# Large loads asked for by GpSimd's software queue, one packet per DMA engine, in place of SyncE's hardware queue

## The chip, the cores and the metric

The kernel runs on one core of a Trainium2 chip. The metric is the device time of one execution in microseconds (us): 1309.09 us for the kernel before, the median of 3 runs (1309.06 to 1309.27). Times inside an execution are counted from the first instruction of the span that the profiler recorded.

## The reference, cut to what matters

Decode step of a block with cached keys and values, B = 4 batches, 32 heads, 4096 cached positions, head size 128, model width 512, all in float32:

```python
q = (x @ wq) as (b, h, 1, d)
scores = einsum("bhqd,bhkd->bhqk", q, k_cache) * 128 ** -0.5
o = einsum("bhqk,bhkd->bhqd", softmax(scores), v_cache)
a = o as (b, 1, 4096) @ wo
ffn = (gelu(x @ w_gate) * (x @ w_up)) @ w_down        # F = 1792
g = sigmoid((x * gate_w).sum(-1))
return g * a + (1 - g) * ffn
```

The two caches are 268 MB each and every byte of them is read once; with the weights some 565 MB come in, and 8 KB go out.

## The kernel before

The work is cut into NT = 32 turns, one for each batch and group of four heads. A turn needs one K tile and one V tile, each of 128 partitions by 64 KB (8.4 MB): a partition holds 128 consecutive cache rows of one head. All of it lives in one big SBUF tensor, `big`, in which the K tiles of two turns overlap in a quarter of their rows and V has one place.

In turn i, VectorE (DVE) multiplies the shared quarter of the K tile by the query (`products(i, True)`, L384) and sums it (`sums(i, True)`, L390). That quarter is then free, and K of turn i+1 is asked for. DVE goes on with the other three quarters (L384 and L390 again, three times as long), then the row maximum (`soft_max`). ScalarE makes the exponentials (L402). TensorE multiplies V of the turn before by them (`pv(i - 1)`, L416), after which V of turn i is asked for.

Ahead of the turns stands an opening: `wq` (8.4 MB) and K of turn 0 are asked for by SyncE (SP), `x` and `gate_w` (8 KB each) by ScalarE's queue. GpSimd (POOL) makes an identity (`ident`, L298 and L299); TensorE turns `x` with it (`x_turn`, L312), DVE spreads it into `xT` (L317), TensorE projects it with `wq` (`q_project`, L330), DVE picks what it needs out of it (L347 to L368), TensorE and ScalarE spread it (L372, L374) as `qb`, and only then can turn 0 start. `w_gate` and `w_up` (3.7 MB each, `load_f`) go to the place of `wq` in `big`, and are asked for when `q_project` has read it. After the turns come `w_down`, `wo` and the last projections (L497, L505), and SP stores the result in two parts (L616).

Order and waits are set by a small class, `Plan`: each step is recorded with what it reads and writes, in program order, and each engine plays its own steps in that order, with semaphore waits worked out from the overlaps. A load waits on its issuing engine for whoever read its destination last. A load counts its completion on a semaphore of its lane, and its reader waits for that.

The opening loads are played inside a critical section of the tile framework, and then the framework's context is closed, ahead of everything else:

```python
with tc.tile_critical(sync_engine=mybir.EngineType.Pool, no_gpsimd_drain=True):
    plan.play(plan.steps[:opening])
tc.close()
```

Closing the context (its instructions bear the line L625) puts a drain into every engine's program, which is an instruction that holds the engine until its own older work is complete, and a barrier that all five engines enter and leave together. The rows of POOL named `ISA [waits barrier...gather]` below belong to it. So no engine begins `ident`, `ones`, `x_turn` or anything later before each engine has come to that barrier.

Of the kernel before, what the change touches and what calls it, by code (L numbers as in the profile page):

```python
# [19 lines left out]
class Plan:  # L20
# [18 lines left out]
    def add(self, engine, emit, reads=(), writes=(), lane=None, unit=1):  # L39
        lane = lane or engine  # L40
        self.units[lane] = unit
        row = self.by_lane.setdefault(lane, [])
        step = Step(lane, engine, emit, self.turn if engine in self.loops else None)
        step.at = len(row)
        need = {}
        for accesses, writing in ((reads, False), (writes, True)):
            for name, lo, hi in accesses:
                for other, a, b, wrote in self.past.get(name, ()):
                    if a < hi and lo < b and (wrote or writing):
                        if other.lane == engine and engine == "pe":  # L50
                            continue
                        if other.lane == engine and not wrote:
                            continue
                        need[other.lane] = max(need.get(other.lane, -1), other.at)
        seen = self.seen[engine]
        for l, n in sorted(need.items(), key=lambda x: -len(self.by_lane[x[0]])):
            if seen.get(l, -1) >= n:
                continue
            other = self.by_lane[l][n]
            other.asked = True  # L60
            step.waits[l] = n
            seen[l] = n
            for k, v in self.knew[other].items():
                seen[k] = max(seen.get(k, -1), v)
        step.waits = {l: n for l, n in step.waits.items()
                      if not any(self.knew[self.by_lane[m][k]].get(l, -1) >= n for m, k in step.waits.items() if m != l)}
        self.knew[step] = dict(seen)
        self.knew[step][lane] = step.at
        if row and lane == engine:
            for k, v in self.knew[row[-1]].items():  # L70
                if k != lane:
                    self.knew[step][k] = max(self.knew[step].get(k, -1), v)
        for accesses, writing in ((reads, False), (writes, True)):
            for name, lo, hi in accesses:
                old = self.past.get(name, [])
                if writing:
                    old = [x for x in old if not (lo <= x[1] and x[2] <= hi)]
                self.past[name] = old + [(step, lo, hi, writing)]
        row.append(step)
        self.steps.append(step)  # L80
        return step
# [51 lines left out]
def tile_gated_mix(tc: tile.TileContext, x, kc, vc, wq, wo, w_gate, w_up, w_down, gate_w, out):  # L133
    nc = tc.nc
# [108 lines left out]
    add = plan.add  # L243
    V, A, T, G = nc.vector, nc.scalar, nc.tensor, nc.gpsimd
# [11 lines left out]
        return g if plan.k is None else plan.k  # L256

    def load(dst, src, writes, lane):
        return add("sp", lambda: nc.sync.dma_start(dst, src), (), writes, lane=lane, unit=16)

    def load_kv(kind, i):
        src = (vc, kc)[kind == "k"]
        a = KB_ * (i % 2) if kind == "k" else VA if i < NT - 1 else 0
        s = src[i % B, HT * (i // B):HT * (i // B) + HT].rearrange("h (p r) d -> (h p) (r d)", p=PH)
        load(place(a, TW), s, [z(a, TW)], "vl" if kind == "v" and i == NT - 1 else kind)
# [7 lines left out]
    def load_f(s):  # L273
        load(place((F0, F1)[s], KC * F), (w_gate, w_up)[s].rearrange("(p c) n -> p (c n)", c=KC),
             [z((F0, F1)[s], KC * F)], f"f{s}")

    def load_d():
        load(place(D0, FC * DM), w_down.rearrange("(p i) n -> p (i n)", i=FC), [z(D0, FC * DM)], "k")
# [326 lines left out]
    for h in range(2):  # L605
# [4 lines left out]
        for c, move in ((2 * h + 1, act), (2 * h, dve)):  # L610
            dst, read, write = res[:B, slice(*COLS[c])], [(("acc", "po0")[h], 0, C4)], [("res", *COLS[c])]
# [46 lines left out]
```

## Time and profile before

| what | before |
|---|---|
| median of 3 runs | 1309.09 us |
| span of the profiled execution | 1307.7 us (its time around the span is not listed; the median is 1.4 us above the span) |
| DVE busy | 1158.2 us, 89% |
| TensorE busy | 354.1 us, 27% |
| ScalarE busy | 87.3 us, 7% |
| POOL busy | 0.7 us, 6 instructions |
| SP's DMA queue | 10960 packets, 564.67 MB, 99.7% of 16 engines' time |
| mean DMA rate | 432 GB/s over the span |

A busy share is a mean over the span. The DMA share is that of the 16 DMA engines together; DMA-issuing instructions are not counted as busy, and show in the timeline as `SPq`, the sequencer of SP. In a row of the timeline stand the start, the time taken, the engine, the line, the operation, what it writes and reads, how many instructions are merged in the row, and in brackets how long the engine stood idle before it and what ended that.

### The profile page before, as it was taken

To read this page: it belongs to the slowest core of one execution; us is meant where nothing else is said; L and a number is where in the kernel's file an instruction comes from. 1 tells how busy PE (TensorE), PEld (TensorE's weight loads), DVE (VectorE), ACT (ScalarE), POOL (GpSimd) and SP (SyncE) were. 2 spreads that over 40 slices of the span, in tenths; PEclk is the share of its full clock that TensorE was granted. 3 is DMA by queue.
4 is the path that set the end of the run, shared out by engine and by line. 5 is a ranking of instruction groups with operands and counts; after the bars stand their busy time and mean duration, and the time that the engine had idled before them with its cause. 6 is when DMAs were issued, how large, how long until landed. Compare 5 with 4: busy or idle time off the path is not lost.

```text
span 1307.7 us, 6169 instructions
## 1 busy us (share of the span) xinstructions
PE 354.1 (27%) x2512; PEld 100.8 (8%) x2512; DVE 1158.2 (89%) x303; ACT 87.3 (7%) x291; POOL 0.7 (0%) x6
## 2 busy tenths in 40 slices
PE   3402233201332211322221223321133322122227
PEld 0100001000010000100000000100001000000002
DVE  1899999999899998989989888998989898898992
ACT  0000000000000000000000000000000000000001
POOL 0000000000000000000000000000000000000000
PEclk9656666556666556666656666665666665576669
DMA  9999999999999999999999999999999999999998
GB/s 417 417 446 427 440 439 425 443 425 443 427 441 425 441 425 441 431 437 439 427 443 425 443 427 441 425 441 425 441 431 437 439 427 443 425 443 427 439 428 370
DMA packets 10986, 564.83 MB, mean 432 GB/s; under 512 B 1232, under 2 KB 1752, under 8 KB 1888
## 3 DMA queue, kind: packets, MB, share of 16 engines
q1 hardware_dynamic: 10960, 564.67, 99.7%
q8 instruction: 7, 0.11, 0.0%
q10 hardware_dynamic: 16, 0.02, 0.0%
q14 instruction: 3, 0.02, 0.0%
HBM read 564.67 MB, written 0.01 MB: 432 GB/s over the span
## 4 chain that ended last, share of the span: by engine, by line
DMA 71%; DVE 28%; issue 1%; PE 0%; ACT 0%; SPq 0%; DVEq 0%; POOLq 0%
DMA big<-in_A_k_cache 69%; DVE big L384 14%; DVE sc L390 13%; DMA big<-in_A_wo 2%; PE acc L505 0%; PE wide L497 0%; PE po L505 0%; DVE hT L537 0%; DVE big L535 0%; DVE big L534 0%; DVE big L532 0%; ACT big L511 0%; DVE m L395 0%; ACT big L533 0%; DVE big L530 0%
## 5 line engine op out<-in xcount | busy, mean ns | idle before, releaser
L384 DVE TENSOR_TENSOR big<-big,qb 128x4096 f32<-128x4096 f32 x64 | 556.0, 8687 | 88.8 <-DMA big<-in_A_k_cache 88.8
L390 DVE TENSOR_REDUCE sc<-big 128x32 f32<-128x4096 f32 x64 | 555.9, 8686 | 2.3
L416 PE MATMUL po<-big,PM 128*32 128x512 f32 x2048 | 293.4, 737 | 903.1 <-DMA big<-in_A_v_cache 903.1
L416 PEld LDWEIGHTS po<-big,PM 128*32 128x32 f32 x2048 | 72.3, 132 | 1117.8 <-DMA big<-in_A_v_cache 825.2
L402 ACT ACTIVATE PM<-sc,nb 32x128 f32<-32x128 f32 x128 | 67.2, 525 | 476.5 <-DVE nb L397 429.0
L424 ACT ACTIVATE o<-po 128x512 f32<-128x512 f32 x16 | 9.6, 597 | 443.9 <-PE po L416 443.9
L402 ACT ACTIVATION_READ_ACCUMULATOR PM<-sc,nb 32x1 f32 x128 | 26.1, 204 | 0.0
L374 ACT ACTIVATE qb<-q 128x512 f32<-128x512 f32 x8 | 4.8, 597 | 249.6 <-PE q L372 249.6
L347 DVE TENSOR_TENSOR big<-po,amask 128x512 f32<-128x512 f32 x2 | 1.3, 686 | 19.3 <-PE po L330 19.3
L433 PE MATMUL sm<-o,sel 128*16 128x128 f32 x128 | 15.4, 273 | 5.8 <-ACT o L424 5.8
L330 PE MATMUL po<-big,xT 128*32 128x512 f32 x64 | 10.0, 793 | 18.6 <-DMA big<-in_A_wq 18.6
L518 PE MATMUL q<-big,xT 128*32 128x448 f32 x64 | 10.8, 848 | 13.7 <-DMA big<-in_B_w_gate 11.0
L433 PEld LDWEIGHTS sm<-o,sel 128*16 128x16 f32 x128 | 11.7, 97 | 14.4 <-ACT o L424 13.1
L615 DVE COPY res<-acc 4x144 f32<-4x144 f32 x1 | 0.3, 296 | 13.2 <-PE acc L505 13.2
L372 PE MATMUL q<-QM,hc 128*128 128x512 f32 x16 | 9.9, 706 | 4.2 <-DVE hc L368 4.2
L395 DVE TENSOR_REDUCE m<-sc 128x1 f32<-128x128 f32 x32 | 9.2, 286 | 1.1
L440 DVE RECIPROCAL ri<-sm 16x1 f32<-16x1 f32 x8 | 1.2, 156 | 8.2 <-PE sm L435 8.2
L396 DVE STREAM_TRANSPOSE mt<-m 128x32 f32<-128x32 f32 x32 | 6.8, 212 | 1.1
L397 DVE TENSOR_REDUCE nb<-mt 128x1 f32<-128x32 f32 x32 | 6.0, 186 | 1.1
L497 PE MATMUL wide<-big 128*32 128x512 f32 x46 | 5.6, 596 | 2.3 <-DMA big<-in_A_wo 2.3
L518 PEld LDWEIGHTS q<-big,xT 128*32 128x32 f32 x64 | 3.3, 159 | 20.5 <-issue 20.5
L330 PEld LDWEIGHTS po<-big,xT 128*32 128x32 f32 x64 | 2.7, 139 | 25.1 <-issue 25.1
(74 smaller groups left out, 58.3 us busy)
## 6 DMA issues: line engine op xcount, KB each, us to landing
big<-in_A_wo SPq DMA_DIRECT2D x1, 4096.0 KB, 28.7
big<-in_B_w_gate SPq DMA_DIRECT2D x1, 3584.0 KB, 17.6
big<-in_B_w_up SPq DMA_DIRECT2D x1, 3584.0 KB, 25.8
big<-in_B_w_down SPq DMA_DIRECT2D x1, 3584.0 KB, 19.4
big<-in_A_wo SPq DMA_DIRECT2D x1, 1792.0 KB, 26.3
big<-in_A_wo SPq DMA_DIRECT2D x1, 1280.0 KB, 29.0
big<-in_A_k_cache SPq DMA_DIRECT2D x32, 29.7
big<-in_A_v_cache SPq DMA_DIRECT2D x32, 29.4
```

Of the source, the lines that this page charges most:

```text
L330: last = T.matmul(PO[s][32 * j:32 * j + 32].rearrange("p j d -> p (j d)"), xTf[:, c, :32], w[:, n0:n0 + HB * D], start=c == 0, stop=c == K ...
L372: pe(lambda: T.matmul(q.rearrange("p b d -> p (b d)"), HC.rearrange("p h k -> p (h k)"), QM.rearrange("p b d -> p (b d)"), start=True, sto ...
L384: dve(lambda: V.tensor_tensor(k, k, QB[:, b:b + 1, :].to_broadcast([P, r1 - r0, D]), op=OP.mult), m + t("qb"), m)
L390: dve(lambda: V.tensor_reduce(SC[i % 2][:, r0:r1], k, axis=AX.X, op=OP.add), [z(KA(i) + r0 * D, (r1 - r0) * D)], [(f"sc{i % 2}", r0, r1)])
L395: dve(lambda: V.tensor_reduce(M1[n], SC[n], axis=AX.X, op=OP.max), t(f"sc{n}"), t(f"m1{n}"))
L396: dve(lambda: V.transpose(MT, M1[n].to_broadcast([P, PH])), t(f"m1{n}"), t("mt"))
L397: dve(lambda: V.tensor_reduce(NB[n], MT, axis=AX.X, op=OP.max, negate=True), t("mt"), t(f"nb{n}"))
L402: last = A.activation(PM[:, PZ:].rearrange("p (c m) -> p c m", m=32)[s, :, h:RJ * HT:HT], SC[n][s, :].rearrange("p (c j) -> p c j", j=RJ), ...
L416: last = T.matmul(PO[n][32 * c:32 * c + 32].rearrange("p j d -> p (j d)"), PM[:, m0:m0 + 32], place(VAT(i) + j * N, N), start=b == 0 and j ...
L424: act(lambda: A.activation(O[n], PO[n], AF.Copy), t(f"po{n}"), t(f"o{n}"))
L433: T.matmul(sm[:B * HT, :D], selv[:, j, m0:m0 + B * HT], O[n][:, j, :], start=(n, j) == (0, 0), stop=(n, j) == (N - 1, RJ - 1))
L518: last = T.matmul(q.rearrange("p b d -> p (b d)")[32 * j:32 * j + 32, :FG], xTf[:, c, :32], place((F0, F1)[s] + c * F + j * FG, FG), start ...
```

## The change

The helper through which every large load goes asks on another engine, and with another option:

```diff
     def load(dst, src, writes, lane):
-        return add("sp", lambda: nc.sync.dma_start(dst, src), (), writes, lane=lane, unit=16)
+        return add("pool", lambda: G.dma_start(dst, src, single_packet=True), (), writes, lane=lane, unit=16)
```

`wq`, all K and V tiles, `w_gate`, `w_up`, `w_down` and the pieces of `wo` move from SP's hardware queue to POOL's software queue, where GpSimd's own processors write the descriptors. `single_packet=True` asks that what a load gives one DMA engine, here 8 partitions' rows, forms one packet. `x` and `gate_w` stay on ScalarE's queue and the two stores on SP's. The waits of the loads are the same and move with them. PE, DVE and ACT keep their programs.

POOL's program from the start to `ident` and a little beyond, before (`lane_...` are the semaphores of `Plan`, `..._49` and `barrier_...` those of the framework):

```order
L622 NO_OP
L625 UNCONDITIONAL_BRANCH
L622 NO_OP [waits SP_sequencer_49,Activation_sequencer_49,Pool_sequencer_49]
L625 UNCONDITIONAL_BRANCH
L625 ISA [waits barrier_Pool_Activation_PE_DVE_SP_gather]
L298 MEMSET ident 128x128 [waits barrier_Pool_Activation_PE_DVE_SP_gather]
L299 ISA [waits lane_pool]
L299 AFFINE_SELECT ident<-ident 128x128
```

and the same place after:

```order
L259 DMA big<-in_A_wq 128x16384
L259 DMA big<-in_A_k_cache 128x16384
L622 UNCONDITIONAL_BRANCH
L622 NO_OP [waits Pool_49]
L622 NO_OP [waits Activation_sequencer_49,Pool_sequencer_49]
L625 UNCONDITIONAL_BRANCH
L625 ISA [waits barrier_Pool_Activation_PE_DVE_SP_gather]
L298 MEMSET ident 128x128 [waits barrier_Pool_Activation_PE_DVE_SP_gather]
L299 ISA [waits lane_pool]
L299 AFFINE_SELECT ident<-ident 128x128
L259 DMA big<-in_B_w_gate 128x7168 [waits lane_pe]
L259 DMA big<-in_B_w_up 128x7168
```

POOL now comes to the drain and the barrier of the closed context with two 8.4 MB loads of its own behind it, and the later loads stand behind `ident` on it.

SP's program at the same place before:

```order
L259 DMA big<-in_A_wq 128x16384
L259 DMA big<-in_A_k_cache 128x16384
L622 UNCONDITIONAL_BRANCH
L625 UNCONDITIONAL_BRANCH [waits Pool_49]
L259 DMA big<-in_B_w_gate 128x7168 [waits SP_sequencer_49,Activation_sequencer_49,Pool_sequencer_49,barrier_Pool_Activation_PE_DVE_SP_release,lane_pe]
L259 DMA big<-in_B_w_up 128x7168
L259 DMA big<-in_A_k_cache 128x16384 [waits lane_dve]
L259 DMA big<-in_A_v_cache 128x16384 [waits lane_dve]
```

and all of SP's after:

```order
L654 UNCONDITIONAL_BRANCH
L625 UNCONDITIONAL_BRANCH x2
L616 DMA out<-res 4x288 [waits Activation_sequencer_49,Pool_sequencer_49,Pool_49,barrier_Pool_Activation_PE_DVE_SP_release,lane_fin0]
L616 DMA out<-res 4x224 [waits lane_fin1]
L635 ISA [waits lane_out]
```

What is left on SP are the two stores; each load's own wait (`lane_pe`, `lane_dve`) is POOL's now.

## The prediction

> **What bounds the kernel now.** I read the page's first parts, then the windows, then the timeline at three places.
>
> ```profile
> span 1307.7 us, 6169 instructions
> q1 hardware_dynamic: 10960, 564.67, 99.7%
> 281.00:1200.00 919.00, 238.52 (x1656) 65.46 (x1656) 843.98 (x184) 61.33 (x210) 0.00 (x0) 0.62 1.00 434
> DMA 71%; DVE 28%; issue 1%; PE 0%; ACT 0%; SPq 0%; DVEq 0%; POOLq 0%
> ```
>
> The second row is SP's queue: its packets take 99.7% of the 16 DMA engines' span. The third is a window of 919 us in mid-run, whose last two columns are the DMA share (1.00) and GB/s (434). The kernel is bound by the bytes it moves, and nothing but an idle or a slower DMA stream can lengthen it much. So I ask of each issue: how much was still queued ahead of it when it was made?
>
> ```profile
> 543.39 4.43 DVE L384 TENSOR_TENSOR big<-big,qb 128x4096 f32<-128x4096 f32 x1 [2.14 <-DMA big<-in_A_k_cache]
> 552.18 12.95 DVE L384 TENSOR_TENSOR big<-big,qb 128x12288 f32<-128x12288 f32 x1
> 552.30 0.33 SPq L259 DMA_DIRECT2D big<-in_A_k_cache  x1
> 562.72 9.73 PE L416 MATMUL po<-big,PM 128*32 128x512 f32 x64 [27.38 <-DMA big<-in_A_v_cache]
> 572.51 0.33 SPq L259 DMA_DIRECT2D big<-in_A_v_cache  x1
> 582.04 4.43 DVE L384 TENSOR_TENSOR big<-big,qb 128x4096 f32<-128x4096 f32 x1 [3.13 <-DMA big<-in_A_k_cache]
> ```
>
> One turn lasts 582.04 - 543.39 = 38.65 us. K is asked for at 552.30, while the V ahead of it lands at 562.72: a cover of 10.4 us. V is asked for at 572.51 and the K ahead lands at 582.04: 9.5 us. An issue may be some microseconds slower here without an idle DMA engine. The opening has no such cover everywhere:
>
> ```profile
> 0.89 0.40 SPq L259 DMA_DIRECT2D big<-in_A_wq  x1
> 1.35 0.42 SPq L259 DMA_DIRECT2D big<-in_A_k_cache  x1
> 2.87 0.20 POOL L298 MEMSET ident<- 128x128 f32 x1 [2.43 <-POOLq L625]
> 2.97 0.17 DVE L301 MEMSET ones<- 128x128 f32 x1 [2.97 <-PEq L625]
> 5.39 0.89 DVE L317 COPY xT<-sg 128x128 f32<-128x128 f32 x4
> 10.67 0.68 DVE L320 TENSOR_TENSOR big<-big 4x512 f32<-4x512 f32 x1 [4.39 <-DMA big<-in_gate_w]
> 22.88 9.99 PE L330 MATMUL po<-big,xT 128*32 128x512 f32 x64 [18.58 <-DMA big<-in_A_wq]
> 32.93 0.33 SPq L259 DMA_DIRECT2D big<-in_B_w_gate  x1
> 39.16 0.60 ACT L374 ACTIVATE qb<-q 128x512 f32<-128x512 f32 x1 [35.00 <-PE q L372]
> 42.15 4.43 DVE L384 TENSOR_TENSOR big<-big,qb 128x4096 f32<-128x4096 f32 x1 [5.16 <-DMA big<-in_A_k_cache]
> 51.06 0.33 SPq L259 DMA_DIRECT2D big<-in_A_k_cache  x1
> 59.19 1.45 PE L518 MATMUL q<-big,xT 128*32 128x448 f32 x8 [2.64 <-DMA big<-in_B_w_up]
> 69.48 0.33 SPq L259 DMA_DIRECT2D big<-in_A_v_cache  x1
> 92.16 0.33 SPq L259 DMA_DIRECT2D big<-in_A_k_cache  x1
> 99.17 9.39 PE L416 MATMUL po<-big,PM 128*32 128x512 f32 x64 [35.07 <-DMA big<-in_A_v_cache]
> ```
>
> All engines leave the closing barrier (L625) at 2.9 us, though SP's two loads have only been asked for: wq lands just before 22.88, K at 42.15. Behind that the chain is ident, xT (done at 5.39 + 0.89 = 6.28), q_project (22.88 to 32.87), and w_gate is asked for at 32.93, with 9.2 us of K still to come. That chain fits under the first two loads only because the barrier opens early.
>
> **The change, part by part.**
>
> *Dropped on SP, added on POOL: 74 issues.* SP's issues take 0.33 to 0.43 us each and SP waits anyway. POOL is idle (0.7 us busy in all), so the waits have nothing behind them but the next load. No row shows a software issue. I call its extra time to the first byte L and take 1.0 us, two to three times SP's issue, since POOL's own instructions (0.20 above) are short. Ends: -0.4 (SP's 0.40 falls away and nothing comes for it) and 2.5, a second start-up as long as the present one. The present one follows from
>
> ```profile
> big<-in_A_wq SPq DMA_DIRECT2D x1, 21.8
> big<-in_B_w_gate SPq DMA_DIRECT2D x1, 3584.0 KB, 17.6
> ```
>
> wq lands 21.8 us after its issue; 8.39 MB at 434 GB/s are 19.3 us, so 2.5 us are start and completion. In the turns L is covered by 9.5 and 10.4 us: cost nothing; if a load needed more than some 7 us (9.5 - 2.5), each microsecond beyond would be paid up to 64 times. The Trainium skill (DMA: Bandwidth & Descriptors, Specifications) gives about 1 us to the first byte for the software path and 0.6 for the hardware path; L would be 0.4 by it, and the sum below 17.7 instead of 18.9. No run here shows it yet.
>
> *The barrier, the term that decides.* POOL now holds wq and K when it comes to the drain of the closed context. What a drain does with a software load in flight no row of before shows: POOL had none. Ends: it passes once the descriptors are written (cost L, hidden under the 18.58 us that q_project waited), or it holds until both have landed. SP's passing at 2.9 us is for a hardware queue, which took the load off SP's hands; POOL's software keeps the account of its own loads, and a drain is there to hold an engine until older work is done. I take the landing. Then:
>
> - K lands at 42.15 + L. From the end of its issue (1.77) to ident the barrier took 2.87 - 1.77 = 1.10: engines start at 43.25 + L.
> - Start to xT took 6.28 - 2.87 = 3.41: 46.66 + L. wq, x and gate_w are long there, so q_project runs at once, 9.99: 56.65 + L. gate_w's chain on DVE (from 10.67 in before) fits beside it.
> - w_gate is asked for 0.06 later, at 56.71 + L. The DMA engines have been idle since K landed.
> - w_gate and w_up are 2 x 3.67 MB, 16.9 us at 434, plus 2.5 plus L from an idle start: w_up lands at 76.1 + 2L, against 59.19. The DMA stream is late by 16.9 + 2L.
>
> Does the stream stay unbroken? DVE had `qb` at 39.76 and waited for K until 42.15. Now q_project ends 23.78 + L later, so `qb` comes at 63.54 + L, and DVE is late by 21.4 + L, more than the stream. With L = 1: K of turn 1 is asked for at 51.06 + 22.4 = 73.5 and would land from an empty queue at 73.5 + 22.8 = 96.3, behind w_up at 78.1 + 19.3 = 97.4: covered by 1.1. V of turn 0: 91.9 + 22.8 = 114.7 against 97.4 + 19.3 = 116.7: covered by 2.0. K of turn 2: 92.16 + 22.4 + 22.8 = 137.4 against V's landing 99.17 + 18.9 + 19.3 = 137.4: just covered. After that DVE, 3.5 us later than the stream, makes it good out of the 3.13 us that it waits in a turn. So 16.9 + 2 x 1.0 = 18.9 us, once.
>
> *Packets.* One packet of 8 rows, 512 KB, instead of 8 of 64 KB. The rate in mid-run was 434 at a share of 1.00, so nothing stands idle between packets to be won back beyond what rounding hides: half a step, 0.5%, 6.5 us better. Worse I bound by a whole step, 1%, 13 us. I take zero, since the bytes are the same. The Trainium skill (DMA: Bandwidth & Descriptors, Why small descriptors are slow) names a fixed 3 cycles for each packet; over 7/8 of 10960 / 16 packets at 850 MHz that is an estimate of 2 us won, which would bring the sum to 17.
>
> *End.* SP's stores have SP to themselves; they waited for the result, not for SP. Zero.
>
> Sum against the profiled execution: 1307.7 + 18.9 = 1326.6 of span; the runs' median stands 1.4 above the span, so 1309.1 + 18.9 = 1328.0. What can be told from no change is about 0.2%, 2.6 us.
>
> **Rivals.**
>
> 1. The drain passes at issue, not slower. Engines start at 2.87 + L or a little more, q_project still waits for wq, all shifts by L = 1: 1310, from 1303.5 with the rate's better end to about 1316 if gate_w (10.67, already behind wq's packets) waits behind two 19.3 us packets: landing at 42 it would hold DVE until `qb` at some 52, 10 us late, against a cover of 99.17 - 92.16 - 3.5 = 3.5 at K of turn 2. For it: SP's case. Against: the program asks for completion, and this time the loads are POOL's. It decides where ident starts below 25 us, so that q_project still ends under K. The Trainium skill (Perfetto Trace Analysis, Per-engine timelines) lets a software load's instruction end with its last descriptor, with the data still to move; by that rule the drain would pass early.
> 2. DVE locks POOL out while it writes descriptors. K is asked for at 552.30, just when the 12.95 us multiply starts; held until 565.13, K would land at 565.1 + 22.8 = 587.9 instead of 582.04, 5.9 us in each of 31 turns: 183, in all 1511. For it: issue and multiply coincide in every turn. Against: nothing in before, POOL did not work then. The Trainium skill (SBUF — State Buffer, Who interferes with whom) has a multiply with two SBUF inputs collide with POOL's reads but not with its writes, and infers that descriptors need only writes; its trap for software loads is meant for copies of another kind, so by it 1328 stands.
> 3. The software path moves bytes slower: 2.5%, twice and a half my worse bound, adds 32: 1360. Nothing speaks for it but that no row shows that path. That `single_packet` changes nothing would be seen in the packet count alone, at 1328.
>
> **How the numbers follow.** Forecast 81%: 1328. Rival 1 11%, rival 2 4%, rival 3 4%. The forecast's own range: L = -0.4 and the better rate give 1309.1 + 16.1 - 6.5 = 1318.7; L = 2.5 and the worse rate 1309.1 + 21.9 + 13 = 1344. 1318 to 1344 leaves out the other cases (19%) and little more, so it is the range. Rival 1 splits 3 / 6 / 2 in faster, same, slower; all else is slower: 0.03, 0.06, 0.91.
>
> **What would show it.** POOL's ident near 44 us instead of 2.87, q_project near 48 right behind xT with no wait for wq, w_gate asked for near 58, a hole of about 15 us in the DMA share between 43 and 58, and 434 GB/s with 38.65 us a turn from then on. If ident starts near 4 us, the barrier term is wrong and rival 1 holds. If turns are longer than 38.7 us, my cover of the issues or the rate is wrong: a K that is asked for only at the multiply's end is rival 2, one asked for in time that takes longer is rival 3.

## The result, and the profile after

The changed kernel takes 1327.63 us (median, 1327.05 to 1328.06) against 1309.07 us: a ratio of 1.0142, 95% interval 1.0127 to 1.0156. It is slower by 18.6 us; the profiled span went from 1307.7 to 1326.6 us, by 18.9.

The page of the changed kernel: its span, the slices of DMA share (in tenths) and rate, the software queue, and the chain that ended last. Ahead of it stands the row of DMA share from the page of before.

```profile
DMA  9999999999999999999999999999999999999998
```

```profile
span 1326.6 us, 6169 instructions
DMA  9499999999999999999999999999999999999998
GB/s 410 193 440 413 443 441 431 426 439 443 425 433 439 439 421 439 441 439 419 441 441 429 429 439 443 423 435 439 439 421 439 441 437 421 441 441 429 429 435 373
q0 software_dynamic: 10560, 564.66, 98.4%
DMA 66%; DVE 28%; PE 1%; issue 1%; ACT 0%; POOL 0%; DVEq 0%; POOLq 0%
```

Of 40 slices one has changed: in the second the DMA share is 4 tenths and the rate 193 GB/s. In all others the share is the same tenth as before. The opening of its timeline shows why (start, time taken, engine, line, in brackets the idle time before and who ended it):

```profile
1.50 0.67 POOL L259 DMA_DIRECT2D big<-in_A_wq  x1 [1.05 <-PEq L625]
2.16 0.53 POOL L259 DMA_DIRECT2D big<-in_A_k_cache  x1
44.06 0.20 POOL L298 MEMSET ident<- 128x128 f32 x1 [41.37 <-POOLq L625]
44.16 0.17 DVE L301 MEMSET ones<- 128x128 f32 x1 [44.16 <-PEq L625]
46.57 0.88 DVE L317 COPY xT<-sg 128x128 f32<-128x128 f32 x4
47.51 9.30 PE L330 MATMUL po<-big,xT 128*32 128x512 f32 x64 [2.03 <-DVE xT L317]
57.16 0.55 POOL L259 DMA_DIRECT2D big<-in_B_w_gate  x1 [12.37 <-PE po L330]
77.43 3.21 PE L518 MATMUL q<-big,xT 128*32 128x448 f32 x16 [3.51 <-DMA big<-in_B_w_up]
114.02 0.53 POOL L259 DMA_DIRECT2D big<-in_A_k_cache  x1 [22.15 <-DVE sc L390]
117.02 8.68 PE L416 MATMUL po<-big,PM 128*32 128x512 f32 x64 [33.75 <-DMA big<-in_A_v_cache]
```

POOL has asked for both loads by 2.7 us and then does nothing for 41.37 us; it is held at L625, the closed context. What holds it there is one instruction. Asked for the instructions of L625, the trace of before lists the drains of POOL and SP so (count, then shortest, median and longest time in ns, then the first and the last start in us):

```profile
L625 POOLq DRAIN  x3: 34/41/60, 2.2 to 2.6; - x3
L625 SPq DRAIN  x3: 7/7/7, 2.2 to 2.5; - x3
```

In the changed kernel POOL's drains, and the time from the issue to the landing of K of turn 0, are:

```profile
L625 POOLq DRAIN  x3: 40/78/41153, 2.2 to 43.8; - x3
big<-in_A_k_cache POOLq DMA_DIRECT2D x1, 41.1
```

One drain starts at 2.2 us and takes 41.15 us, so it ends at 43.4; its record shows no semaphore that it waits for. K, asked for at 2.16, lands 41.1 us later, at 43.3. In before the drains of SP took 7 ns, with the same two loads of its own in flight. With POOL the barrier holds DVE, PE and ACT; `ident` starts at 44.06 instead of 2.87. q_project no longer waits for wq but for xT, and w_gate is asked for at 57.16, when the DMA engines have been empty for some 14 us. Windows of the same run (busy time of the engines, then granted clock, DMA share, GB/s):

```profile
43.00:59.00 16.00, 9.94 (x68) 2.82 (x68) 7.53 (x25) 1.28 (x1) 1.56 (x4) 1.00 0.10 23
300.00:1219.00 919.00, 239.01 (x1656) 65.66 (x1656) 844.05 (x184) 61.33 (x210) 25.37 (x48) 0.63 1.00 434
```

Between 43 and 59 us the share is 0.10: 14.4 us of idle DMA. In 919 us of mid-run the share is 1.00 and the rate 434 GB/s, the same figures as before. One turn there:

```profile
562.45 4.42 DVE L384 TENSOR_TENSOR big<-big,qb 128x4096 f32<-128x4096 f32 x1 [2.12 <-DMA big<-in_A_k_cache]
571.24 12.95 DVE L384 TENSOR_TENSOR big<-big,qb 128x12288 f32<-128x12288 f32 x1
571.62 0.53 POOL L259 DMA_DIRECT2D big<-in_A_k_cache  x1 [18.64 <-DVE sc L390]
581.79 8.41 PE L416 MATMUL po<-big,PM 128*32 128x512 f32 x64 [27.00 <-DMA big<-in_A_v_cache]
601.13 4.43 DVE L384 TENSOR_TENSOR big<-big,qb 128x4096 f32<-128x4096 f32 x1 [3.17 <-DMA big<-in_A_k_cache]
```

The turn takes 601.13 - 562.45 = 38.68 us (38.65 before). POOL's issue starts 0.38 us behind the 12.95 us multiply, runs beside it in 0.53 us, and K lands on time.

### The profile page after: what moved, and what is told of

It is laid out like the page before. It is cut to its first block, busy times and chain, and to the rows that moved or that the text cites. A ratio compares the mean times of both kernels' runs of the same rounds, so it can differ in the third digit from the quotient of the medians.

```text
span 1326.6 us, 6169 instructions
## 1 busy us (share of the span) xinstructions
PE 355.0 (27%) x2512; PEld 100.6 (8%) x2512; DVE 1158.2 (87%) x303; ACT 87.4 (7%) x291; POOL 41.0 (3%) x82
## 2 busy tenths in 40 slices
DMA packets 10602, 564.83 MB, mean 426 GB/s; under 512 B 1232, under 2 KB 1240, under 8 KB 1504
## 4 chain that ended last, share of the span: by engine, by line
DMA 66%; DVE 28%; PE 1%; issue 1%; ACT 0%; POOL 0%; DVEq 0%; POOLq 0%
DMA big<-in_A_k_cache 64%; DVE big L384 14%; DVE sc L390 13%; DMA big<-in_A_wo 2%; PE po L330 1%; PE acc L505 0%; PE q L372 0%; PE wide L497 0%; DVE big L350 0%; DVE big L347 0%; PE po L505 0%; DVE hT L537 0%; DVE PM L307 0%; DVE xT L317 0%; DVE big L535 0%
## 5 line engine op out<-in xcount | busy, mean ns | idle before, releaser
L259 POOL DMA_DIRECT2D big<-in_A_v_cache x32 | 16.9, 528 | 601.1 <-PE po L416 564.9
L259 POOL DMA_DIRECT2D big<-in_A_k_cache x32 | 16.9, 529 | 575.1 <-DVE sc L390 575.1
L433 PEld LDWEIGHTS sm<-o,sel 128*16 128x16 f32 x128 | 11.7, 97 | 14.4 <-ACT o L424 13.1
## 6 DMA issues: line engine op xcount, KB each, us to landing
big<-in_B_w_down POOLq DMA_DIRECT2D x1, 3584.0 KB, 18.6
```

The source lines that it names most:

```text
L259: return add("pool", lambda: G.dma_start(dst, src, single_packet=True), (), writes, lane=lane, unit=16)
L433: T.matmul(sm[:B * HT, :D], selv[:, j, m0:m0 + B * HT], O[n][:, j, :], start=(n, j) == (0, 0), stop=(n, j) == (N - 1, RJ - 1))
```

## The experiments

Two theories were tried against each other: that the whole loss comes from POOL's drain at the closed context, waiting for POOL's own loads to land; or that the software path or its packets cost something in the run at large.

**The opening back on SP.** The loads of the opening get lanes of their own (`q0`, `k0`) and an engine by lane; everything else is as in the changed kernel.

```diff
     def load(dst, src, writes, lane):
+        if lane in ("q0", "k0"):
+            return add("sp", lambda: nc.sync.dma_start(dst, src), (), writes, lane=lane, unit=16)
         return add("pool", lambda: G.dma_start(dst, src, single_packet=True), (), writes, lane=lane, unit=16)
```

> wq and K of turn 0 go back to SP; all other loads stay on POOL as single packets. My theory (the whole cost is POOL's drain at the closed context, which waits for the landing of the loads that POOL itself has asked for): POOL has nothing in flight there, ident starts near 2.9 us instead of 44.06, q_project waits for wq again, no hole in the DMA stream; 1309.1 us, within 0.2% of before, since the longer issue is covered by 9 us and more in each turn. Rival, the software path itself costs (its rate, or 72 longer issues): most of the 18.6 us stays, 1320 to 1328.

Measured: 1310.15 us, ratio to before 1.0008 (0.9999 to 1.0017). 97% of the bytes still go through POOL, and the loss is gone. Its timeline:

```profile
2.88 0.20 POOL L300 MEMSET ident<- 128x128 f32 x1 [2.43 <-POOLq L627]
22.97 9.60 PE L332 MATMUL po<-big,xT 128*32 128x512 f32 x64 [18.68 <-DMA big<-in_A_wq]
32.92 0.68 POOL L260 DMA_DIRECT2D big<-in_B_w_gate  x1 [29.31 <-PE po L332]
45.45 4.42 DVE L386 TENSOR_TENSOR big<-big,qb 128x4096 f32<-128x4096 f32 x1 [8.76 <-DMA big<-in_A_k_cache]
50.75 5.51 PE L520 MATMUL q<-big,xT 128*32 128x448 f32 x32 [11.40 <-DMA big<-in_B_w_gate]
```

ident and q_project are back where they were, and POOL's drains take at most 60 ns again, with SP's 16.8 MB in flight. One thing moved: K of turn 0 lands just ahead of 45.45 instead of 42.15, though nothing was late in asking for it. w_gate now stands in another queue than K, and is served beside it instead of behind it. So DVE starts turn 0 3.3 us later, and K of turn 2 is asked for at 95.73 instead of 92.16, with only 3.3 us left of the V ahead of it:

```profile
95.73 0.53 POOL L260 DMA_DIRECT2D big<-in_A_k_cache  x1 [22.15 <-DVE sc L392]
99.05 9.11 PE L418 MATMUL po<-big,PM 128*32 128x512 f32 x64 [35.12 <-DMA big<-in_A_v_cache]
```

The median lies 1.0 us above before, with an interval that just includes no difference. The trace has this microsecond at K of turn 2. A load is split among the 16 DMA engines, and each of them counts its part when it is done. The mean of the 16 parts comes within 0.02 us of before for w_up, K of turn 1 and V of turn 0, but 0.93 us later for K of turn 2, and from K of turn 3 on 1.0 to 1.1 us later.

**The converse: only the opening on POOL.**

```diff
     def load(dst, src, writes, lane):
-        return add("pool", lambda: G.dma_start(dst, src, single_packet=True), (), writes, lane=lane, unit=16)
+        if lane in ("q0", "k0"):
+            return add("pool", lambda: G.dma_start(dst, src, single_packet=True), (), writes, lane=lane, unit=16)
+        return add("sp", lambda: nc.sync.dma_start(dst, src), (), writes, lane=lane, unit=16)
```

> The converse: only wq and K of turn 0 on POOL, all other loads back on SP's hardware queue. My theory: the drain holds until both have landed, ident near 44 us, the same hole of about 15 us; 1327.4 us, at most 0.5 us below the changed kernel (w_gate's first byte comes sooner from SP). Rival, software path in the turns: near 1309 to 1312.

Measured: 1327.16 us, ratio 1.0141 (1.0125 to 1.0156). ident starts at 43.73:

```profile
43.73 0.21 POOL L300 MEMSET ident<- 128x128 f32 x1 [41.05 <-POOLq L627]
55.67 0.40 SPq L261 DMA_DIRECT2D big<-in_B_w_gate  x1
```

Two of POOL's 76 loads (76, not the 74 that the prediction counted) give the whole loss; the other 74 give at most the microsecond of the run before.

**Without single_packet.**

```diff
-        return add("pool", lambda: G.dma_start(dst, src, single_packet=True), (), writes, lane=lane, unit=16)
+        return add("pool", lambda: G.dma_start(dst, src), (), writes, lane=lane, unit=16)
```

> The changed kernel without single_packet. My theory: the packets carry none of the cost, DMA records still take 2418 ns for 64 KB; 1327.6 us, within 0.2% of the changed kernel. Rival, long packets cost or win something (my bounds were 6.5 us won, 13 us lost): 1315 to 1334.

Measured: 1328.22 us (1327.01 to 1329.84), ratio to before 1.0147 (1.0131 to 1.0162), which overlaps the changed kernel's. A cost or a gain of the option is not seen in the time; one below some 2 us could hide in these intervals. The queue's row in its page is the same to the last packet, so the trace does not show that the option changed the transfers at all:

```profile
q0 software_dynamic: 10560, 564.66, 98.4%
```

The 400 packets fewer than in before come with POOL's queue and not with the option: both pages count 1240 packets under 2 KB, where the page of before counts 1752.

**All on POOL, but behind the closed context.**

```diff
     with tc.tile_critical(sync_engine=mybir.EngineType.Pool, no_gpsimd_drain=True):
-        plan.play(plan.steps[:opening])
+        plan.play([s for s in plan.steps[:opening] if s.engine == "act"])
     tc.close()
     tc.compile()
+    plan.play([s for s in plan.steps[:opening] if s.engine != "act"])
```

> The changed kernel with wq and K of turn 0 asked for by POOL behind the closed context instead of ahead of it; every load is still on POOL as a single packet. My theory: the drain finds nothing in flight, engines start near 2.9 us, wq's first byte comes near 4.3 instead of 2.9 us (1.9 in before), no hole; 1309.1 + 2.4 = 1311.5 us (1310.5 to 1313). Rival, any two 8.4 MB loads on POOL ahead of ident delay it whatever stands between: 1327 or more.

Measured: 1312.08 us, ratio 1.0022 (1.0013 to 1.0031).

```profile
3.39 0.67 POOL L259 DMA_DIRECT2D big<-in_A_wq  x1 [2.94 <-POOLq L625]
4.06 0.53 POOL L259 DMA_DIRECT2D big<-in_A_k_cache  x1
4.58 0.22 POOL L298 MEMSET ident<- 128x128 f32 x1
25.83 9.66 PE L330 MATMUL po<-big,xT 128*32 128x512 f32 x64 [19.81 <-DMA big<-in_A_wq]
```

The same two loads stand ahead of ident on the same engine, and ident follows them at once; the drains, now ahead of the loads, take at most 67 ns. What held POOL is not the loads but the drain behind them. Most of the price that is left is the later start: q_project, which waits for wq, begins at 25.83 instead of 22.88, 2.95 us later, and the medians differ by as much (1312.08 - 1309.13). The profiled run is the slowest of the ten (1313.02), so the agreement to the last digit is chance.

**Only wq ahead of the closed context.**

```diff
     with tc.tile_critical(sync_engine=mybir.EngineType.Pool, no_gpsimd_drain=True):
-        plan.play(plan.steps[:opening])
+        plan.play(plan.steps[:opening - 1])
     tc.close()
     tc.compile()
+    plan.play(plan.steps[opening - 1:opening])
```

> The changed kernel with only wq ahead of the closed context and K of turn 0 behind it, both on POOL. My theory (the drain waits for the landing of what POOL has asked for by then, no more): it holds until wq has landed, some 23.3 us; K of turn 0 is asked for near 24.2 and its first byte comes near 25.6, against wq's last near 22.3: a hole of 3.3 us. ident near 25.4, q_project 28.5 to 38, w_gate asked for near 38 with K still running: no second hole. 1309.1 + 1.0 + 3.3 = 1313.4 us (1312 to 1315). Rival, the wait has a fixed length or depends on something else: ident again near 44 us and 1327, or 1311 without any wait.

Measured: 1314.25 us, ratio 1.0040 (1.0026 to 1.0055).

```profile
1.50 0.67 POOL L259 DMA_DIRECT2D big<-in_A_wq  x1 [1.05 <-PEq L625]
25.06 0.53 POOL L259 DMA_DIRECT2D big<-in_A_k_cache  x1 [22.89 <-POOLq L625]
25.58 0.22 POOL L298 MEMSET ident<- 128x128 f32 x1
39.24 0.55 POOL L259 DMA_DIRECT2D big<-in_B_w_gate  x1 [12.92 <-PE po L330]
47.35 4.43 DVE L384 TENSOR_TENSOR big<-big,qb 128x4096 f32<-128x4096 f32 x1 [4.32 <-DMA big<-in_A_k_cache]
L625 POOLq DRAIN  x3: 40/67/21762, 2.2 to 24.3; - x3
```

With half as much in flight the hold is about half as long (22.89 us instead of 41.37), and the drain in it takes 21.76 us instead of 41.15. w_gate is asked for 8 us ahead of K's landing, so there is no second hole; K lands 5.2 us later than in before, and the time is longer by 5.1.

**wq alone on POOL, K in SP's queue beside it.**

```diff
-        if lane in ("q0", "k0"):
+        if lane == "q0":
```

(against the kernel with only the opening on POOL)

> wq alone on POOL, as a single packet; K of turn 0 and all other loads on SP's hardware queue. By my theory the drain waits for wq alone, so this run shows when wq lands beside K in the other queue. If the DMA engines alternate between the two queues row by row (64 KB each), as they did in the kernel with the opening on SP, wq lands near 41 us, ident comes near 42.5, and the time is 1324 to 1327. If what single_packet asks for, 8 rows in one piece, held against the other queue, wq would land near 25.5, ident near 27, w_gate would be asked for before K's end, and the time would be 1309.5 to 1311.5.

Measured: 1325.71 us, one run.

```profile
0.90 0.40 SPq L261 DMA_DIRECT2D big<-in_A_k_cache  x1
1.47 0.66 POOL L260 DMA_DIRECT2D big<-in_A_wq  x1 [1.02 <-PEq L627]
42.87 0.20 POOL L300 MEMSET ident<- 128x128 f32 x1 [40.74 <-POOLq L627]
55.19 0.35 SPq L261 DMA_DIRECT2D big<-in_B_w_gate  x1
big<-in_A_k_cache SPq DMA_DIRECT2D x1, 38.8
big<-in_A_wq POOLq DMA_DIRECT2D x1, 40.7
L627 POOLq DRAIN  x3: 34/60/40036, 2.2 to 42.6; - x3
```

wq took 22.5 us from its issue to its landing in the changed kernel, and takes 40.7 beside K. K, in SP's queue, lands at 0.90 + 38.8 = 39.7 us; wq lands at 1.47 + 40.7 = 42.2, and the drain, 40.04 us long from 2.2 on, ends at 42.2. So it waits for POOL's own load, and not for K. The records of the transfers show how wq came to be so late: of the rows of 64 KB that start between 12 and 14 us 16 are POOL's, of those that start between 14 and 16 us 16 are SP's, and so on. The 16 engines serve the two queues in turn, one row of 2.42 us at a time, though single_packet was asked for.

All runs in one table; the time follows what POOL has in flight when it drains, and when that lands:

| POOL's loads in flight at the drain | ident starts | time |
|---|---|---|
| none (before) | 2.87 | 1309.1 |
| none; opening on SP | 2.88 | 1310.2 |
| none; opening behind the context | 4.58 | 1312.1 |
| wq alone, nothing beside it | 25.58 | 1314.3 |
| wq, with K beside it in SP's queue (one run) | 42.87 | 1325.7 |
| wq and K, all else on SP | 43.73 | 1327.2 |
| wq and K, no single_packet | 43.86 | 1328.2 |
| wq and K (the changed kernel) | 44.06 | 1327.6 |

## Why the prediction was right

- *The barrier term.* The choice between the two ends, passing at issue or at landing, decided, and landing is what was seen: ident at 44.06 (44.25 worked out). The drain's own record (41.15 us), the run behind the context and the ones with wq alone show that it is the drain, and that it lasts until POOL's loads have landed. The load's own instruction on POOL is over in 0.53 to 0.67 us, with the data still to move; it is the drain behind it that is not. The first rival is out: nothing behind the barrier starts before 44 us.
- *The sum.* 18.9 was forecast and 18.9 of span measured, but that they agree to 0.1 us is luck: two errors of a microsecond cancelled. w_up landed at 77.43 instead of 78.1 (q_project took 9.30, not 9.99), and V of turn 0 came 17.85 us later than before where 18.9 was worked out. The rest was lost afterwards: the shift of V's landing is 17.94 in the next turn and 18.85 in the one after that, and 19.07 at mid-run (581.79 against 562.72). The last rows for this, before and then after:

```profile
137.77 8.87 PE L416 MATMUL po<-big,PM 128*32 128x512 f32 x64 [29.20 <-DMA big<-in_A_v_cache]
176.37 10.04 PE L416 MATMUL po<-big,PM 128*32 128x512 f32 x64 [29.73 <-DMA big<-in_A_v_cache]
```

```profile
155.71 9.81 PE L416 MATMUL po<-big,PM 128*32 128x512 f32 x64 [30.00 <-DMA big<-in_A_v_cache]
195.22 8.84 PE L416 MATMUL po<-big,PM 128*32 128x512 f32 x64 [29.70 <-DMA big<-in_A_v_cache]
```

  The step that was too kind is K of turn 2, "just covered". The parts of the 16 DMA engines show it. Their mean is later than in before by 0.89 us for K of turn 0, by 17.82 for w_up, 17.84 for V of turn 0, 18.86 for K of turn 2, and by 18.87 to 18.96 from there to the last turns. So the later first load cost 0.9 us, the hole 16.9, and K of turn 2 another 1.0; forecast were 1.0, 17.9 and nothing. K of turn 2 was asked for at 114.02, 3.0 us ahead of V's landing. But the last row of that V ends on 14 of the 16 engines between 114.7 and 115.2 us already, and only on the slowest at 116.7. The rows of K start from 115.2 on, the last at 116.7, and most of the first ones take 2.9 to 3.5 us instead of 2.4. The landing of the last part hides this at first, because the engines finish K of turn 2 closer together (from 135.50 to 136.34 us; in before from 116.55 to 118.43).
- *L.* The last part of wq lands at 23.97 instead of 22.74, 1.2 us later, where 1.0 was taken: POOL comes to its first issue 0.6 us later than SP did, at 1.50, and the load takes 0.6 us longer from there. In the turns it costs nothing, as the same 38.7 us a turn and the run with the opening on SP show.
- *Packets at zero.* Held: 434 GB/s before and after, and the run without the option. The estimate of 2 us won by fewer packets was not seen, and the trace counts as many packets without the option as with it.
- *The lock between DVE and POOL.* Not there: the issue runs beside the multiply. The third rival, a slower software path, is out by the rate and by the run with the opening on SP.

## What to carry to other kernels

Before a load is moved to GpSimd, look for every drain between its issue and its landing: in these runs GpSimd's drain lasted until the load had landed, and with a barrier behind it all engines waited along. Where the stream of transfers bounds a kernel, the price is not the length of that wait (41 us here) but the hole that it leaves in the stream, so follow it to the next transfer that is asked for too late. Count the cover of a load to the first DMA engine that runs dry, and not to the landing of the last part ahead: here 3 us of cover were a microsecond short. If GpSimd must issue first loads, issue them behind the last drain, at the price of the later start (3 us here).

## What the runs showed of the hardware

- A drain on GpSimd waits for the landing of GpSimd's own software-queued loads: it took 41.15 us with 16.8 MB in flight, 21.76 us with 8.4 MB, and at most 60 ns with 16.8 MB in flight from SP. SP's own drains took 7 ns with 16.8 MB of its own in flight.
- A software issue of 8.4 MB takes POOL 0.53 to 0.67 us (SP: 0.33 to 0.42), also beside a running DVE multiply.
- A hardware and a software queue with work at the same time share the DMA engines row by row (2.42 us for one of 64 KB): K of turn 0 lands 3.3 us later when w_gate stands in the other queue, and wq, asked for at 1.47 with single_packet, lands at 42.2 us beside K.
- The 16 DMA engines do not finish a load together: for V of turn 0 in the changed kernel 14 of them end their last row between 114.7 and 115.2 us, the slowest at 116.7, and the slowest sets the landing.
